# A fused attention and gated-MLP kernel: MLP groups reordered, their later steps emitted one to three groups behind, loads moved to a period's end, four result buffers for two

## Chip, cores and metric

One core of one Trainium2 chip. The metric is device microseconds of one execution of the whole kernel. Engines: PE (TensorE) multiplies, PEld loads its weights, DVE (VectorE), ACT (ScalarE) and POOL (GpSimd) do elementwise work, SP (SyncE) only issues DMAs. Each engine takes its instructions in the order in which they stand in its own queue, and waits on semaphores for those of other engines.

## What is computed

Block-causal attention over 8 batches and 8 heads (576 tokens, head size 64, blocks of 64 tokens), whose output is the input of a gated MLP with a spatial (token by token) product:

```python
scores = scale * np.matmul(q, k.transpose(0, 1, 3, 2))
scores = np.where(mask, scores, -1000000000.0)
attn = np.exp(scores - np.max(scores, axis=-1, keepdims=True))
attn = attn / (np.sum(attn, axis=-1, keepdims=True) + 1e-09)
x = np.matmul(attn, v)                       # then heads side by side: (batch, 576, 512)
h = np.maximum(x @ w_in, 0.0)                # w_in: 512 x 1024
u, v = (h[..., : d_ff // 2], h[..., d_ff // 2 :])
v_n = (v - mu) / np.sqrt(var + 1e-06)        # mean and variance over the 512 channels
v_s = np.einsum('ts,bsd->btd', w_spatial, v_n) + b_spatial[None, :, None]
out = (u * v_s) @ w_out                      # w_out: 512 x 512
```

## The kernel before

Attention is done in pairs of heads, four pairs to a batch, 32 in all. The first batch's four pairs run while the weights are prepared. From then on the program is a loop over the other 28 pairs, and one turn of it is called a **period** here: four periods to a batch, named first to fourth. In a period stand the scores of the pair (`scores_8` for the last 64 tokens, `scores_run` for the rest: matmul into PSUM, mask and maximum on DVE, L476, exponential on ACT, L483, scaling by the reciprocal sum on POOL, L497), the product with v of the pair before (`av_pair`, whose result is split into a rounded high part by ACT, L395, and a low part by DVE, L396), and the turning of this pair's probabilities: DVE transposes 32x32 blocks into `pb` (L556 to L565) and eight DMAs on SP regroup them into `ptt` (L574), for the next period's product.

Between these, PE works off a queue of **MLP groups** of the batch before (`moe`). A credit of `G_PAIR` per period says how many: one group after `scores_8`, the others behind `av_pair`, each followed by up to three steps of the turning. The operands are split into a high and a low fp32r part, and a product is made of three. A batch has 29 groups, each an accumulation in one of the two PSUM banks of `ps_m`:

- **v groups** (`mv`), 5: 128 tokens by 512 channels. ACT applies relu (L623), DVE makes mean and variance (L639, L640), ACT a logarithm and an exponential for the inverse root (L641, L642), DVE refines it (L643 to L655), ACT scales (L659) and casts the high part `vh` (L665), POOL makes the low part `vl` (L666). The fifth, the **tail group**, has the last 64 tokens, whose operand `xs` POOL copies together (`tail_evac`, L409), from both halves of all four pairs; its result is copied by ACT (L634), added by DVE (L635).
- **u groups** (`mu`), 8: two halves of the tokens (z) by four channel blocks; ACT applies relu into the tile `u` (L691).
- **spatial groups** (`ms`), 8: DVE multiplies the result by u (L716), ACT casts the high part `gh` (L717), POOL makes the low part `gl` (L718).
- **result groups** (`mo`), 8: ACT copies the result into a buffer `o` (L736), SP stores it.

With every group, all that follows its matmuls is written directly behind them. PE keeps the order written (every matmul is tied to the one before); on the other engines the framework's scheduler sets the order when the program is built, from its own estimates of when each instruction can run. The order of groups and the two loads of a later pair stand here:

```python
order = "vuvuvuvuvuuuu" if b else "v" * 5 + "u" * 8
groups = [(vs if w == "v" else us).pop(0) for w in order]
for z in range(2):
    groups += [(G_SP, lambda z=z, d=d: sp_group(z, d)) for d in range(ND)]
    groups += [(G_OUT, lambda z=z, e=e: out_group(z, e)) for e in range(NO)]
```

So the first period of a batch has the tail group first, then u and v groups by turns; the second the rest of v and u and one spatial group; the third three spatial groups of the first half, its four result groups, and one spatial group of the second half; the fourth the rest. The last batch's groups run alone at the end.

## Time and profile before

| | |
|---|---|
| runs (3) | 817.1, 817.97 (median), 818.67 us |
| profiled execution | 819.96 us, span 818.1 us |
| PE busy, matmuls | 718.9 us (88%) |
| DVE, ACT, POOL busy | 456.6, 383.7, 288.5 us |
| granted PE clock, mean | 0.954 |
| a batch's four periods | 99 us |
| regroup DMAs `ptt`, stores `outT`, loads of q and k, of v | 224, 64, 31, 32 |

How to read the lines below: in the list of waits, "PE mv L231 <- POOL xs L409: 24.4, 7, 4.0" says that PE stood idle 24.4 us, in 7 places, at most 4.0 us, before matmuls into `mv`, until POOL's instruction of line 409. In the timeline a row is start, duration, engine, line, operation, out<-in, form, count, and in brackets the idle time of its engine ahead of it and what ended that. Most matmuls are made by one helper, so their line is L231; the tile names tell them apart. Their durations overlap: starts, not durations, tell the rate.

### The profile page before, as it was taken

The page shows a single profiled execution, that of the slowest core. Times are in us where ns is not written, and L with a number is a line of the kernel's source. Part 1 is how long each engine was busy: PE and PEld are TensorE (multiplying, and loading weights), DVE is VectorE, ACT ScalarE, POOL GpSimd, SP SyncE. Part 2 cuts the span into 40 slices and gives each one's busy share as a digit, 9 for nine tenths or more (in the row PEclk, how much of TensorE's full clock was granted, in tenths as well). Part 3 has the DMA queues.
Part 4 walks back from the last instruction along what each step waited for, and adds up shares of the span by engine and source line. Part 5 has one row for each costly group of instructions (what it writes and reads, how often), then busy time and mean ns, then how long its engine had stood idle before and what let it go on. Part 6 is the DMA issues. An engine that isn't in the chain of part 4 may idle for free.

```text
span 818.1 us, 14375 instructions
## 1 busy us (share of the span) xinstructions
PE 718.9 (88%) x4864; PEld 609.0 (74%) x4864; DVE 456.6 (56%) x1739; ACT 383.7 (47%) x1088; POOL 288.5 (35%) x444
## 2 busy tenths in 40 slices
PE   8987898978989889888898798887987989879998
PEld 5545787767877678777787688776877868778897
DVE  7967763567525665356654555555654566535420
ACT  6776642446424564344543455343643447423532
POOL 5865543224313234232343313342142423323121
PEclk9999999989999999999999999999999999999999
DMA  5543564551446434463443534536346362353001
GB/s 201 170 143 102 156 172 114 148 136 51 124 112 165 118 83 120 112 166 87 114 118 100 157 81 128 141 79 160 92 97 157 97 165 70 81 126 93 18 8 51
DMA packets 53661, 94.42 MB, mean 115 GB/s; under 512 B 5970, under 2 KB 43346, under 8 KB 53588
## 3 DMA queue, kind: packets, MB, share of 16 engines
q1 hardware_dynamic: 53588, 93.52, 42.9%
q8 instruction: 38, 0.62, 0.3%
q14 instruction: 35, 0.29, 0.1%
HBM read 38.18 MB, written 9.44 MB: 58 GB/s over the span
## 4 chain that ended last, share of the span: by engine, by line
PE 36%; DVE 25%; ACT 11%; SPq 8%; DMA 8%; POOL 6%; issue 5%; DVEq 0%; POOLq 0%; ACTq 0%
PE mu L231 9%; SPq L574 8%; PE mv L231 8%; DVE pb L563 7%; ACT p L483 7%; DVE p L476 7%; PE ms L231 6%; DMA outT<-o 6%; PE s L231 5%; POOL p L497 5%; PE mo L231 4%; DVE sst L491 2%; DVE pb L556 2%; DVE x L396 2%; ACT vr L659 1%
## 5 line engine op out<-in xcount | busy, mean ns | idle before, releaser
L497 POOL TENSOR_SCALAR p<-p,sst 128x384 f32<-128x384 f32 (+4 forms) x252 | 137.0, 560 | 194.7 <-DVE sst L494 117.9
L483 ACT ACTIVATE p<-p,sst 128x384 f32<-128x384 f32 (+4 forms) x252 | 145.0, 577 | 53.6 <-DVE sst L476 52.4
L476 DVE CUSTOM_DVE_ANT_0 p<-s,mask 128x384 f32<-128x384 f32 (+4 forms) x252 | 114.3, 471 | 58.8 <-PE s L231 58.6
L231 PE MATMUL mu<-x,wi_hi 128*128 128x288 f32 x512 | 126.0, 328 | 17.2 <-ACT u L691 16.7
L231 PE MATMUL s<-raw 64*128 64x256 f32 (+4 forms) x640 | 126.5, 440 | 3.4 <-DVE nmax L291 1.8
L231 PEld LDWEIGHTS mu<-x,wi_hi 128*128 128x128 f32 x512 | 96.7, 215 | 21.2 <-ACT u L691 18.7
L716 DVE TENSOR_TENSOR u<-ms,u 128x288 f32<-128x288 f32 x64 | 28.0, 437 | 148.0 <-PE ms L231 148.0
L231 PEld LDWEIGHTS s<-raw 64*128 64x128 f32 (+1 forms) x640 | 73.2, 188 | 41.9 <-issue 19.8
L718 POOL TENSOR_TENSOR gl<-u,gh 128x288 fp32r<-128x288 f32 x64 | 51.4, 803 | 149.9 <-ACT gh L717 148.9
L563 DVE STREAM_TRANSPOSE pb<-p 128x384 f32<-128x384 f32 (+2 forms) x224 | 98.3, 455 | 8.7 <-POOL p L497 7.0
L231 PE MATMUL ms<-ws_hi,vh 128*128 128x288 f32 x256 | 83.8, 327 | 19.7 <-ACT o L736 19.7
L231 PE MATMUL mo<-gh,wo_hi 128*128 128x288 f32 x256 | 73.7, 308 | 23.0 <-DVE u L716 19.6
L231 PE MATMUL mv<-wi_hi,x 128*128 128x512 f32 x256 | 89.9, 414 | 3.4 <-ACT vr L623 3.3
L231 PE MATMUL av<-ptt,v 128*64 128x32 f32 (+4 forms) x1120 | 87.7, 306 | 2.8 <-DVE sst L476 2.7
L666 POOL TENSOR_TENSOR vl<-vr,vh 128x512 fp32r<-128x512 f32 x32 | 41.1, 1286 | 134.4 <-ACT vh L665 134.4
L231 PEld LDWEIGHTS av<-ptt,v 128*64 128x64 f32 x1120 | 75.6, 137 | 15.8 <-DVE sst L476 4.8
L736 ACT COPY o<-mo 128x288 f32<-128x288 f32 x64 | 25.4, 399 | 120.8 <-DMA outT<-o 64.9
L231 PE MATMUL ms<-ws_hi,vl 128*128 128x288 f32 x256 | 78.7, 308 | 0.0
L231 PE MATMUL ms<-ws_lo,vh 128*128 128x288 f32 x256 | 78.6, 307 | 0.0
L231 PE MATMUL mu<-x,wi_lo 128*128 128x288 f32 x256 | 77.9, 322 | 0.0
L717 ACT CAST gh<-u 128x288 fp32r<-128x288 f32 x64 | 27.6, 432 | 106.4 <-DVE u L716 106.4
L231 PE MATMUL mo<-gh,wo_lo 128*128 128x288 f32 x256 | 70.9, 297 | 0.0
(120 smaller groups left out, 1308.9 us busy)
## 6 DMA issues: line engine op xcount, KB each, us to landing
ptt<-pb SPq DMA_DIRECT2D x224, 200.0 KB, 4.1
raw<-qk SPq DMA_DIRECT2D x31, 608.0 KB, 4.0
v<-v SPq DMA_DIRECT2D x32, 320.0 KB, 3.0
outT<-o SPq DMA_DIRECT2D x64, 144.0 KB, 2.1
rwi<-w_in SPq DMA_DIRECT2D x8, 512.0 KB, 3.6
rwo<-w_out SPq DMA_DIRECT2D x4, 512.0 KB, 4.1
rws<-w_spT SPq DMA_DIRECT2D x4, 288.0 KB, 2.8
rwt<-w_spT SPq DMA_DIRECT2D x2, 144.0 KB, 4.2
```

The source lines that it names most:

```text
L231: ins = nc.tensor.matmul(out, lhsT, rhs, start=start, stop=stop).ins
L396: nc.vector.tensor_tensor(out=lo, in0=av, in1=hi.bitcast(F32), op=ALU.subtract)
L476: nc.vector.tensor_tensor_reduce(out=p[:, at:at + n], in0=ps, in1=mk, scale=-0.125, scalar=BIG if m == 0 else st[:, k:k + 1], op0=ALU.add, ...
L483: nc.scalar.activation(p, p, AF.Exp, bias=mx, scale=-1.0, accum_out=st[:, 10 + k:11 + k])
L497: nc.gpsimd.tensor_scalar(out=p, in0=p, scalar1=st[:, k:k + 1], scalar2=1.0, op0=ALU.mult, op1=ALU.mult)
L563: nc.vector.transpose(to(hd * XH + 32 * t, [[P, m], *dims] if m > 1 else dims), p[:, :m * P])
L574: nc.sync.dma_start(ptts[(b, pr)][:, a, xs], pb[32 * a:32 * a + 32, :, xs])
L666: nc.gpsimd.tensor_tensor(out=vl, in0=vr, in1=vh.bitcast(F32), op=ALU.subtract)
L716: nc.vector.tensor_tensor(out=uz, in0=ps[:, :HT], in1=uz, op=ALU.mult)
L717: nc.scalar.copy(gh[:, dc, :], uz)
L718: nc.gpsimd.tensor_tensor(out=gl[:, dc, :], in0=uz, in1=gh[:, dc, :].bitcast(F32), op=ALU.subtract)
L736: nc.scalar.copy(o, ps[:, :HT])
```

## The change

1. The v groups are made in the order 0, 1, tail, 2, 3 (before: tail, 0, 1, 2, 3). The last u group moves behind the four spatial groups of the first half.
2. Each group becomes a generator. When a group is issued, its matmuls and first step are emitted, and then every group still open advances by one step. So a v group's statistics, its root, and its scaling and casts are emitted one, two and three groups behind its relu; a spatial group's `gh` and `gl` one group behind its multiply, but for the fourth, which emits its cast at once and has its low part made by DVE.
3. A result group takes the last quarter of its inputs (k = 3) last, in all three products.
4. The loads of the next pair's v and of the second next pair's q and k stand at a period's end.
5. Four result buffers for two.

```diff
-    o_p = ctx.enter_context(tc.tile_pool(name="o_p", bufs=2))
+    o_p = ctx.enter_context(tc.tile_pool(name="o_p", bufs=4))
...
 # v_group
+            yield
             nc.vector.bn_stats(out=st[:m, 0:6], in_=vr[:m, :])
             nc.vector.bn_aggr(out=st[:m, 6:8], in_=st[:m, 0:6])
+            yield
             nc.scalar.activation(st[:m, 8:9], st[:m, 7:8], AF.Ln, bias=eps[:m, :])
...
+            yield
             nc.scalar.activation(
                 vr[:m, :], vr[:m, :], AF.Identity, bias=st[:m, 13:14], scale=st[:m, 12:13]
             )
...
 # u_group
             nc.scalar.activation(u_tile()[:, dc, zs], ps[:, :HT], AF.Relu)
+            yield
...
 # sp_group
             nc.vector.tensor_tensor(out=uz, in0=ps[:, :HT], in1=uz, op=ALU.mult)
+            if dc < ND - 1:
+                yield
             nc.scalar.copy(gh[:, dc, :], uz)
-            nc.gpsimd.tensor_tensor(
+            (nc.vector if dc == ND - 1 else nc.gpsimd).tensor_tensor(
                 out=gl[:, dc, :], in0=uz, in1=gh[:, dc, :].bitcast(F32), op=ALU.subtract
             )
+            if dc == ND - 1:
+                yield
...
 # out_group
-            for a, ws in ((gh, (wo_hi, wo_lo)), (gl, (wo_hi,))):
-                for k in range(ND):
-                    for w in ws:
+            for ks in (range(ND - 1), (ND - 1,)):
+                for a, w in ((gh, wo_hi), (gh, wo_lo), (gl, wo_hi)):
+                    for k in ks:
...
-        vs = [(G_V if c < FULL else G_VT, lambda c=c: v_group(c)) for c in (FULL, 0, 1, 2, 3)]
+        vs = [(G_V if c < FULL else G_VT, lambda c=c: v_group(c)) for c in (0, 1, FULL, 2, 3)]
...
-        for z in range(2):
-            groups += [(G_SP, lambda z=z, d=d: sp_group(z, d)) for d in range(ND)]
-            groups += [(G_OUT, lambda z=z, e=e: out_group(z, e)) for e in range(NO)]
+        groups = groups[:-1] + [(G_SP, lambda d=d: sp_group(0, d)) for d in range(ND)] + groups[-1:]
+        groups += [(G_OUT, lambda e=e: out_group(0, e)) for e in range(NO)]
+        groups += [(G_SP, lambda d=d: sp_group(1, d)) for d in range(ND)]
+        groups += [(G_OUT, lambda e=e: out_group(1, e)) for e in range(NO)]
...
+    def issue(f):
+        gen = f()
+        next(gen)
+        for e in list(behind):
+            if next(e, e) is e:
+                behind.remove(e)
+        behind.append(gen)
...
-            f()
+            issue(f)
...
-        if g + 1 < len(pairs):
-            load_v(*pairs[g + 1])
-        if g + 2 < len(pairs):
-            load_pair(*pairs[g + 2])
         n = max(n, g * NT)
         while group():
...
         for f in rest:
             f()
+        if g + 1 < len(pairs):
+            load_v(*pairs[g + 1])
+        if g + 2 < len(pairs):
+            load_pair(*pairs[g + 2])
```

How the change moves instructions shows in three places (names: tile, batch, number of the group; `x_4_3` is pair 3 of batch 4). First ACT in a batch's first period, from the split of the last pair's product on; before:

```order
L395 CAST x_4_3_4931<-av_4_3_0_4920 128x288
L395 CAST x_4_3_4931<-av_4_3_1_4934 128x288
L634 COPY vr_4_4_4953<-mv_4_4_4952 64x512
L691 ACTIVATE u_4_4998<-mu_4_0_0_4985 128x288
L641 ACTIVATE st_4_4_4954<-st_4_4_4954,eps_113 64x1
L642 ACTIVATE st_4_4_4954<-st_4_4_4954 64x1
L659 ACTIVATE vr_4_4_4953<-vr_4_4_4953,st_4_4_4954 64x512
L623 ACTIVATE vr_4_0_5008<-mv_4_0_5007 128x512
L672 CAST vs_a_123<-vr_4_4_4953 64x512
```

and now:

```order
L395 CAST x_4_3_4931<-av_4_3_0_4920 128x288
L395 CAST x_4_3_4931<-av_4_3_1_4934 128x288
L623 ACTIVATE vr_4_0_4949<-mv_4_0_4948 128x512
L643 ACTIVATE st_4_0_4950<-st_4_0_4950,eps_113 128x1
L694 ACTIVATE u_4_4984<-mu_4_0_0_4971 128x288
L644 ACTIVATE st_4_0_4950<-st_4_0_4950 128x1
L662 ACTIVATE vr_4_0_4949<-vr_4_0_4949,st_4_0_4950 128x512
L668 CAST vh_4_0_5036<-vr_4_0_4949 128x512
L623 ACTIVATE vr_4_1_4996<-mv_4_1_4995 128x512
```

The tail group's copy (L634) has left the place behind the split; v 0's relu stands there, u's relu now between the logarithm (L643) and the exponential (L644), and v 1's relu behind v 0's cast.

Next DVE in a third period, from the last row sums of the softmax on; before:

```order
L494 RECIPROCAL sst_4_2_4371<-sst_4_2_4371 128x4
L396 TENSOR_TENSOR x_4_1_4461<-av_4_1_0_4450,x_4_1_4461 128x288
L563 STREAM_TRANSPOSE pb_4_2_4500<-p1_4_2_0_4434 128x2x4x32
L396 TENSOR_TENSOR x_4_1_4461<-av_4_1_1_4464,x_4_1_4461 128x288
L563 STREAM_TRANSPOSE pb_4_2_4500<-p1_4_2_0_4434 128x4x32
L565 STREAM_TRANSPOSE pb_4_2_4500<-p3_4_2_1_4417 128x4x32
L563 STREAM_TRANSPOSE pb_4_2_4500<-p2_4_2_1_4427 128x3x4x32
L716 TENSOR_TENSOR u_3_4002<-ms_3_0_2_4482,u_3_4002 128x288
L563 STREAM_TRANSPOSE pb_4_2_4500<-p1_4_2_1_4439 128x2x4x32
L563 STREAM_TRANSPOSE pb_4_2_4500<-p1_4_2_1_4439 128x4x32
L716 TENSOR_TENSOR u_3_4002<-ms_3_0_3_4507,u_3_4002 128x288
```

and now:

```order
L494 RECIPROCAL sst_4_2_4373<-sst_4_2_4373 128x4
L565 STREAM_TRANSPOSE pb_4_2_4500<-p3_4_2_1_4419 128x4x32
L563 STREAM_TRANSPOSE pb_4_2_4500<-p2_4_2_1_4429 128x3x4x32
L563 STREAM_TRANSPOSE pb_4_2_4500<-p1_4_2_0_4436 128x2x4x32
L563 STREAM_TRANSPOSE pb_4_2_4500<-p1_4_2_0_4436 128x4x32
L563 STREAM_TRANSPOSE pb_4_2_4500<-p1_4_2_1_4441 128x2x4x32
L563 STREAM_TRANSPOSE pb_4_2_4500<-p1_4_2_1_4441 128x4x32
L720 TENSOR_TENSOR u_3_3988<-ms_3_0_3_4480,u_3_3988 128x288
L724 TENSOR_TENSOR gl_3_0_4334<-u_3_3988,gh_3_0_4333 128x288
L396 TENSOR_TENSOR x_4_1_4463<-av_4_1_0_4452,x_4_1_4463 128x288
L396 TENSOR_TENSOR x_4_1_4463<-av_4_1_1_4466,x_4_1_4463 128x288
```

The multiply of the fourth spatial group (L716, now L720) is behind the last transpose in both; the third's has gone ahead of them, and the two splits of x come behind the multiply and the new low part.

Last SP in a third period; before:

```order
L224 DMA raw_5_0_4480<-qk 128x1216
L248 DMA v_4_3_4478<-v 128x640
L574 DMA ptt_4_2_4527<-pb_4_2_4500 128x1x400 x8
L737 DMA outT<-o_3_0_0_4545 128x288
L737 DMA outT<-o_3_0_1_4565 128x288
L737 DMA outT<-o_3_0_2_4586 128x288
L737 DMA outT<-o_3_0_3_4602 128x288
```

and now:

```order
L574 DMA ptt_4_2_4523<-pb_4_2_4500 128x1x400 x7
L746 DMA outT<-o_3_0_0_4541 128x288
L574 DMA ptt_4_2_4523<-pb_4_2_4500 128x1x400
L746 DMA outT<-o_3_0_1_4561 128x288
L746 DMA outT<-o_3_0_2_4582 128x288
L746 DMA outT<-o_3_0_3_4598 128x288
L224 DMA raw_5_1_4857<-qk 128x1216
L248 DMA v_5_0_4855<-v 128x640
```

The loads have moved behind the stores; the first store stands ahead of the last regroup DMA.

## The prediction

> **What bounds the kernel now.** I read the page first, then TensorE's (PE's) waits, then the busy time by period, then the timeline around each wait.

> ```profile
> span 818.1 us, 14375 instructions
> PE 718.9 (88%) x4864; PEld 609.0 (74%) x4864; DVE 456.6 (56%) x1739; ACT 383.7 (47%) x1088; POOL 288.5 (35%) x444
> raw<-qk SPq DMA_DIRECT2D x31, 608.0 KB, 4.0
> ```
> ```profile
> PE mv L231 <- POOL xs L409: 24.4, 7, 4.0
> PE ms L231 <- ACT o L736: 19.7, 7, 3.3
> PE mo L231 <- DVE u L716: 19.6, 14, 2.4
> PE mu L231 <- ACT u L691: 16.7, 7, 2.7
> ```
> PE is the bound: no other engine passes 56%. What it loses stands in four waits, each once (the third twice) per batch: 80.4 us together. The next rows are one batch's four periods in PE's order: third, fourth, then first and second of the next batch (us of the period, then busy time of each engine, clock, DMA).

> ```profile
> 211.52:238.57 27.05, 22.70 (x167) 20.34 (x166) 11.87 (x47) 9.34 (x28) 8.31 (x14) 0.95 0.47 122
> 238.57:259.65 21.08, 19.53 (x151) 17.23 (x150) 11.97 (x47) 8.55 (x26) 8.32 (x14) 0.98 0.45 119
> 259.65:287.24 27.59, 23.48 (x142) 19.06 (x141) 17.36 (x65) 14.54 (x40) 6.42 (x11) 0.94 0.47 121
> 287.24:310.60 23.36, 20.95 (x148) 18.32 (x147) 14.26 (x55) 12.36 (x36) 8.96 (x13) 0.93 0.43 108
> ```
> A batch takes 99 us. The clock column is under 1 in all four, so I cut finer (PE busy, clock):

> ```profile
> 201.88:205.29 3.41, 1.01 (x8) 1.00 0.40 68
> 205.29:208.70 3.41, 3.41 (x17) 0.51 0.84 208
> 222.36:225.77 3.41, 2.10 (x16) 1.00 0.12 16
> 225.77:229.18 3.41, 3.19 (x23) 1.00 0.90 209
> 236.10:239.51 3.41, 3.41 (x14) 0.51 0.25 87
> 273.56:277.00 3.44, 3.44 (x13) 0.51 0.87 204
> ```
> A long wait costs twice: the 3.4 us behind it run at half clock, which loses about 1.6 us of matmuls. After a wait of 2.4 us (1.01 busy) it happens, after one of 1.3 us (2.10 busy) it doesn't. [...] The trace falls already after a window that was 30% busy. [...]

> **The change part by part.** A u group's 12 matmuls take 1.58 us and a v group's 2.77 (0.132 and 0.231 each); a spatial group's 14 are 1.85, the tail group's 8 are 1.85.

> ```profile
> 283.06 1.58 PE mu L231 x12
> 284.63 2.77 PE mv L231 x12
> ```

> *Four result buffers, reordered groups: the third period.*

> ```profile
> 224.06 6.80 SPq L574 DMA_DIRECT2D ptt<-pb  x8
> 224.61 0.42 DVE L716 TENSOR_TENSOR u<-ms,u 128x288 f32<-128x288 f32 x1
> 225.18 0.37 PE L231 MATMUL mo<-gh,wo_hi 128*128 128x288 f32 x1 [1.31 <-DVE u L716]
> 225.50 0.42 DVE L716 TENSOR_TENSOR u<-ms,u 128x288 f32<-128x288 f32 x1
> 227.56 0.29 PE L231 MATMUL mo<-gh,wo_hi 128*128 128x288 f32 x1
> 230.97 5.19 SPq L737 DMA_DIRECT2D outT<-o  x4
> 234.92 0.79 ACT L736 COPY o<-mo 128x288 f32<-128x288 f32 x2 [5.19 <-DMA outT<-o]
> 235.37 0.40 PE L231 MATMUL ms<-ws_hi,vh 128*128 128x288 f32 x1 [2.83 <-ACT o L736]
> ```
> The third result's copy waits for a buffer, the buffer for its store, the store for eight regroup DMAs ahead of it on SP. With four buffers no copy waits inside a batch half, and the next half comes a period later: the 2.83 us go, and the half clock at 236.10. The 1.31 us wait is another: the first result group needs a PSUM bank, and the multiply that frees it stands behind the block transposes on DVE. The change puts a u group (1.58) where a spatial group (1.85) was, but the bank is now that of the fourth spatial group, whose multiply (225.50) is last of all; only what is taken from ahead of it, a multiply and x's subtraction (0.3 to 0.8), brings it forward, less where DVE waits for POOL. I take the start as it was, 225.2 (bounds 224.9 and 225.6), so this wait stays. Then the group runs through in 1.58 instead of 227.56 - 225.18 = 2.38, since its last quarter comes last and DVE makes the low half. Four result groups and one spatial: 225.2 + 6.32 + 1.85 = 233.4, against 238.57: 5.2 us, and 0.45 more for the half clock that reached past 238.57. **Third period: -5.65** (bounds -3.5, if the half clock stays behind the wait that is left, and -7.1 if that wait is gone too).

> *Fourth period*: the same order around the products, so its wait stays; the first result group gains from its last quarter, 0.5 (0 to 0.8). **-0.5.**

> *Tail group third: the first period.*

> ```profile
> 262.46 0.78 ACT L736 COPY o<-mo 128x288 f32<-128x288 f32 x2 [5.33 <-DMA outT<-o]
> 263.14 0.78 ACT L483 ACTIVATE p<-p,sst 128x576 f32<-128x576 f32 x1
> 268.98 0.67 ACT L395 CAST x<-av 128x288 fp32r<-128x288 f32 x2
> 271.43 0.86 DVE L563 STREAM_TRANSPOSE pb<-p 128x384 f32<-128x384 f32 x2
> 272.07 0.51 PE L231 MATMUL mv<-wi_hi,xs 128*128 128x512 f32 x1 [3.75 <-POOL xs L409]
> 272.84 0.58 ACT L634 COPY vr<-mv 64x512 f32<-64x512 f32 x1 [3.20 <-PE mv L231]
> 273.46 0.69 DVE L635 TENSOR_TENSOR vr<-mv,vr 64x512 f32<-64x512 f32 x1 [1.18 <-ACT vr L634]
> ```
> The first v group now needs of the last pair only the first cast at 268.98, at its seventh matmul. That cast comes earlier too: ACT's copies no longer wait 5.33 us for a store, which let the period's first exponential start only at 263.14. How much earlier lies between 0 and 5.33; the nearest row is DVE's own work ahead of the cast, which stays, so I take 0.8. The cast's first half (0.34) is then done at 268.5, and the seventh matmul starts there, not at 272.07: the six ahead of it ended at 272.07 - 3.75 = 268.3, or a little sooner, so the wait is half a microsecond and brings no half clock. Six matmuls of 0.231 later, at 269.9, v ends. What is late next is ACT, which takes its rows in order: relu, logarithm, u's relu, the square root's exponential, scale, cast, and only then the next v's relu. The last batch, where nothing else runs, shows this loop:

> ```profile
> 770.73 0.59 ACT L623 ACTIVATE vr<-mv 128x512 f32<-128x512 f32 x1
> 771.30 0.41 ACT L691 ACTIVATE u<-mu 128x288 f32<-128x288 f32 x1
> 772.30 0.29 ACT L641 ACTIVATE st<-st,eps 128x1 f32<-128x1 f32 x1 [0.58 <-DVE st L640]
> 775.05 0.59 ACT L623 ACTIVATE vr<-mv 128x512 f32<-128x512 f32 x1
> ```
> Relu to logarithm 1.57, logarithm to next relu 2.75; u's relu is hidden behind the statistics there and now stands inside: +0.41. The first v's statistics follow the block transposes (end 272.5), logarithm at 273.5, next relu at 276.65, done 277.25; PE is ready for the tail group, which needs that bank, at 269.9 + 1.58 + 2.77 + 1.58 = 275.8: a new wait of 1.45. Next, v 2 needs the tail group's bank: ACT's copy at 276.65 + 1.57 + 0.41 + 2.1 = 280.75 (the cast, 0.6, is behind it), copy and DVE's add end at 282.05; PE is ready at 277.25 + 1.85 + 1.58 = 280.7: a new wait of 1.35. v 2 ends at 284.8, where it ended at 287.24. **First period: -2.4** (bounds -5.4 without the two waits, and +0.8 if both pass 1.9 us and bring a half clock).

> *Second period.*

> ```profile
> 204.19 0.29 ACT L641 ACTIVATE st<-st,eps 128x1 f32<-128x1 f32 x1 [3.95 <-DVE st L640]
> 204.84 0.40 PE L231 MATMUL mu<-x,wi_hi 128*128 128x288 f32 x1 [2.40 <-ACT u L691]
> ```
> PE waits for u's relu, which stands on ACT behind the logarithm, which waits for statistics that DVE makes after the transposes. The rows stand so after the change too, so this wait and its half clock stay. DVE gets the tail's two splits (about 1.1) at the period's start, and ACT's scale and cast of v 2 leave the exponentials (1.4): **+0.2** (-3.9, wait and half clock gone, to +0.8).

> *The rest.* Loads at the period's end: the same 63 loads, each with a whole period (over 20 us) before its use, against 4.0 us to land; SP's stores and regroup DMAs no longer stand behind them. Nothing, unless a load comes a period late (below). Each half's last low part on DVE: 16 subtractions of about 0.44 in place of POOL's; behind them wait the splits of x, not due for a period. Nothing.

> Sum per batch: -5.65 - 0.5 - 2.4 + 0.2 = -8.35. Batches 1 to 6 run so, beside the attention of the next: -50. Batch 0, among the weights' preparation, has the same waits at other sizes: half of that, -4 (0 to -8.4). Batch 7, alone, has none of the four waits now, and its ACT loop grows from 775.05 - 770.73 = 4.32 to 4.73 against PE's 4.35 for a v and a u group: 0 (-1 to +2). Together -54. The profiled execution took 819.96, 1.9 over its span of 818.1; the median of the runs is 817.97, and 817.97 - 54 = **764 us**.

> **Rivals.** [...] (2) ACT's line is shorter than I make it and the first period's two waits vanish, 6 x 2.8: 747; with the second period's wait gone too, 724. For it: later steps are emitted one to three groups behind; against: the order on ACT, where they stand in the same row. (3) The first period's waits grow past 1.9 us and bring half clocks, 6 x 3.2 = 19: 783. (4) The stores stay the gate: the copies wait again a half later. Then the third period keeps 5.2 of its 5.65: 795. Against: the store issued at 230.97 had landed at 234.92, and its buffer is needed a period, over 20 us, later. (5) **Slower**: a load at the period's end comes late, and every period's first scores wait for it. There are 27 periods; the gain is gone when each waits 2.0 us, that is, when a load lands 22 us after the end of the period before its own; at 3 us each it would be 845. Against: 4.0 us to land.

> **Chances.** My sum 0.55, (1) 0.08, (2) 0.15, (3) 0.12, (4) 0.05, (5) 0.05. A difference under 0.2% (1.6 us) is no change by what such a measurement can tell. Faster 0.94, same 0.01, slower 0.05. The range, 740 to 788, takes in (1), (3) and the nearer half of (2).

> **What would show it.** Right: ACT's results wait for no store; PE's spatial groups for no copy; PE's v groups not for the tail split; half clock once per batch, in the second period; new waits of PE's v groups on ACT's relu and on DVE's add, over 1 us each; the wait on DVE's multiply still there, twice per batch. Wrong: half-clock stretches as many as before, or none; waits on loads; a second period that shortens.

## The result, and the profile after

The changed kernel takes 748.1 us (median of 4, 746.6 to 749.89) against 817.54 before (4 runs): ratio 0.9153, interval 0.9124 to 0.9183, so 8.5% faster. The profiled execution took 749.12 us. The page's first lines after, the head of PE's list of waits, and the four periods of the same batch in the same order as before (third, fourth, then first and second):

```profile
span 747.3 us, 14409 instructions
PE 691.7 (93%) x4864; PEld 583.6 (78%) x4864; DVE 464.9 (62%) x1755; ACT 383.8 (51%) x1088; POOL 276.4 (37%) x428
```
```profile
PE mo L231 <- DVE u L720: 19.9, 14, 2.4
PE mv L231 <- DVE vr L635: 9.9, 8, 3.9
PE mu L231 <- ACT u L694: 8.9, 7, 1.3
PE ms L231 <- ACT u L694: 3.5, 8, 1.5
```
```profile
205.05:226.78 21.73, 20.36 (x164) 18.66 (x163) 12.14 (x47) 9.25 (x28) 6.87 (x13) 1.00 0.49 127
226.78:247.25 20.47, 19.06 (x153) 17.16 (x152) 12.30 (x48) 9.06 (x27) 7.53 (x13) 1.00 0.53 140
247.25:270.34 23.09, 21.99 (x142) 17.46 (x141) 16.44 (x60) 13.21 (x37) 7.70 (x12) 1.00 0.56 149
270.34:292.35 22.01, 20.37 (x149) 17.60 (x148) 15.16 (x61) 13.38 (x38) 8.36 (x13) 1.00 0.45 119
```

A batch takes 87.3 us where it took 99. Two of the four waits are gone from the list (POOL's `xs`, ACT's copy of a result), the wait on u's relu is 1.3 us at most where it was 2.7, the wait on DVE's multiply is as it was. The clock column is 1.00 in all four periods: in each of them a wait of 0.9 to 1.4 us is left, and none brings a half clock. By period, from the start of the first score matmul to the next one's, mean of six batches (the fourth: of five), before to after:

| | predicted | measured |
|---|---|---|
| third period | -5.65 | -5.6 |
| fourth period | -0.5 | -0.5 |
| first period | -2.4 | -4.6 |
| second period | +0.2 | -1.3 |
| all up to the end of batch 0's groups | -4 | +0.7 |
| batch 7 with the last fourth period | -0.5 | -0.1 |

In the row of batch 0, the time up to the third pair's scores is 1.2 us longer (26.56 us for 25.34). That stretch takes 25.0 to 26.7 us in the twelve profiled executions, and differs by 1.1 between the kernel before and the same kernel with four buffers. The rest of the row is 0.5 us shorter.

### The profile page after: what moved, and what is told of

Same layout as the page of the kernel before. It is cut to its first block, busy times and chain, and to the rows that moved or that the text cites. A ratio compares the mean times of both kernels' runs of the same rounds, so it can differ in the third digit from the quotient of the medians.

```text
span 747.3 us, 14409 instructions
## 1 busy us (share of the span) xinstructions
PE 691.7 (93%) x4864; PEld 583.6 (78%) x4864; DVE 464.9 (62%) x1755; ACT 383.8 (51%) x1088; POOL 276.4 (37%) x428
## 4 chain that ended last, share of the span: by engine, by line
DVE 39%; PE 25%; ACT 16%; POOL 8%; issue 6%; DMA 3%; SPq 3%; POOLq 0%; DVEq 0%; ACTq 0%
PE mo L231 12%; DVE pb L563 9%; DVE p L476 8%; ACT p L483 7%; PE ms L231 6%; POOL p L497 4%; DVE st L640 3%; PE s L231 3%; ACT vr L662 3%; SPq L574 2%; DVE pb L556 2%; POOL vl L669 2%; PE mv L231 2%; DVE sst L491 1%; DVE vr L636 1%
## 5 line engine op out<-in xcount | busy, mean ns | idle before, releaser
L497 POOL TENSOR_SCALAR p<-p,sst 128x384 f32<-128x384 f32 (+4 forms) x252 | 136.2, 557 | 203.3 <-DVE sst L494 101.5
L483 ACT ACTIVATE p<-p,sst 128x384 f32<-128x384 f32 (+4 forms) x252 | 145.0, 577 | 47.6 <-DVE sst L476 44.6
L231 PE MATMUL s<-raw 64*128 64x256 f32 (+4 forms) x640 | 127.6, 446 | 2.3 <-DVE nmax L291 1.8
L231 PE MATMUL mu<-x,wi_hi 128*128 128x288 f32 x512 | 113.2, 300 | 8.9 <-ACT u L694 8.9
L231 PEld LDWEIGHTS s<-raw 64*128 64x128 f32 (+1 forms) x640 | 73.6, 191 | 41.0 <-issue 23.3
L231 PE MATMUL mv<-wi_hi,x 128*128 128x512 f32 x256 | 90.2, 414 | 12.5 <-DVE vr L635 9.9
L563 DVE STREAM_TRANSPOSE pb<-p 128x384 f32<-128x384 f32 (+2 forms) x224 | 96.2, 452 | 5.6 <-POOL p L497 4.4
L231 PEld LDWEIGHTS mu<-x,wi_hi 128*128 128x128 f32 x512 | 85.4, 188 | 12.6 <-ACT u L694 10.5
L720 DVE TENSOR_TENSOR u<-ms,u 128x288 f32<-128x288 f32 x64 | 28.2, 441 | 100.3 <-PE ms L231 100.2
L231 PE MATMUL av<-ptt,v 128*64 128x32 f32 (+4 forms) x1120 | 86.8, 306 | 2.3 <-DVE sst L476 2.1
L231 PEld LDWEIGHTS av<-ptt,v 128*64 128x64 f32 x1120 | 77.0, 137 | 13.5 <-DVE sst L476 4.6
L231 PE MATMUL ms<-ws_hi,vh 128*128 128x288 f32 x256 | 80.8, 316 | 3.6 <-ACT u L694 3.5
L231 PE MATMUL ms<-ws_hi,vl 128*128 128x288 f32 x256 | 76.2, 298 | 1.0 <-POOL vl L669 0.3
L724 POOL TENSOR_TENSOR gl<-u,gh 128x288 fp32r<-128x288 f32 x48 | 38.4, 801 | 100.5 <-ACT gh L723 100.5
L231 PE MATMUL mo<-gh,wo_hi 128*128 128x288 f32 x256 | 56.9, 303 | 19.9 <-DVE u L720 19.9
L231 PE MATMUL ms<-ws_lo,vh 128*128 128x288 f32 x256 | 75.3, 294 | 0.0
L231 PEld LDWEIGHTS mv<-wi_hi,x 128*128 128x128 f32 x256 | 49.2, 192 | 28.6 <-DVE vr L635 11.9
L231 PE MATMUL mu<-x,wi_lo 128*128 128x288 f32 x256 | 69.8, 295 | 0.0
## 6 DMA issues: line engine op xcount, KB each, us to landing
raw<-qk SPq DMA_DIRECT2D x31, 608.0 KB, 3.8
```

The lines of the kernel that those rows point to most:

```text
L231: ins = nc.tensor.matmul(out, lhsT, rhs, start=start, stop=stop).ins
L483: nc.scalar.activation(p, p, AF.Exp, bias=mx, scale=-1.0, accum_out=st[:, 10 + k:11 + k])
L497: nc.gpsimd.tensor_scalar(out=p, in0=p, scalar1=st[:, k:k + 1], scalar2=1.0, op0=ALU.mult, op1=ALU.mult)
L563: nc.vector.transpose(to(hd * XH + 32 * t, [[P, m], *dims] if m > 1 else dims), p[:, :m * P])
L720: nc.vector.tensor_tensor(out=uz, in0=ps[:, :HT], in1=uz, op=ALU.mult)
L724: (nc.vector if dc == ND - 1 else nc.gpsimd).tensor_tensor(out=gl[:, dc, :], in0=uz, in1=gh[:, dc, :].bitcast(F32), op=ALU.subtract)
```

## The experiments

Each was timed beside the kernel before on the same chip, and ratios are against that. Between chips the kernel before moved by 0.4%, so small differences are read from the periods, not from medians taken on different chips.

**Two result buffers again.**

```diff
-    o_p = ctx.enter_context(tc.tile_pool(name="o_p", bufs=4))
+    o_p = ctx.enter_context(tc.tile_pool(name="o_p", bufs=2))
```

> The changed kernel with two result buffers again (everything else as changed). Theory A (the stores gate the result copies whenever there are two buffers): the third copy of each half waits again for the first store, which stands behind seven or eight regroup DMAs on SP; PE then waits for that copy in the third period (1.5 to 3 us) and ACT's first exponential comes late at the start of the first period; 2 to 4 us a batch, six batches: 760 to 772 us, take 765, and a wait of PE's spatial group on ACT's copy is back in the list. Theory B (the loads' move and the store ahead of the last regroup DMA have freed the stores, buffers don't matter): 748 us, no such wait.

782.18 us, ratio 0.9564 (0.9512 to 0.9616): 34 us of the gain are gone, and the wait on the copy is back. From PE's list of waits:

```profile
PE ms L231 <- ACT o L745: 16.1, 7, 3.1
PE av L231 <- DVE sst L476: 7.3, 9, 1.2
PE mv L231 <- ACT x L395: 6.7, 6, 1.3
```

Theory A, larger than expected. By the waits, one late store delays three things: the third period's spatial group (2 to 3 us), and at the start of the next first period, through ACT's late exponentials, the product with v (1 us) and the first v group (1.1 us). The third period is 2.3 to 5.0 us longer, the first 1.6 to 2.4.

**Four buffers alone**, in the kernel before.

```diff
-    o_p = ctx.enter_context(tc.tile_pool(name="o_p", bufs=2))
+    o_p = ctx.enter_context(tc.tile_pool(name="o_p", bufs=4))
```

> The kernel before with four result buffers and nothing else changed. Theory A (the buffers alone take the store out of the copies' way, and with it the delay of the exponentials at the start of the first period): the 2.83 us wait of the third period goes with its half clock (4.4 us a batch), and the first period's last cast comes 1.6 us earlier, so its wait for xs falls from 3.75 to about 2.2 us: 6 us a batch, 782 us, no wait on the copy of a result in the list. Theory B (the loads ahead of the stores on SP hold the stores up too, so that four buffers alone do little): 800 us or more, the wait still there. If the first period keeps its 3.75 us: 791 us.

782.27 us, ratio 0.9525 (0.9496 to 0.9553), as theory A had it. No wait on a copy is left. The wait on `xs` is 2.9 us at most where it was 4.0:

```profile
PE mv L231 <- POOL xs L409: 18.6, 7, 2.9
PE mu L231 <- ACT u L691: 17.5, 11, 2.7
```

So one number in one line brings about half of the gain, with everything else as before. That the time met the forecast is partly luck. The wait on `xs` fell to 2.9 us and not to 2.2. And the wait of the second period stayed (2.4 us, 2.7 in one batch), yet its half clock went in four batches of six, while three fourth periods got one behind the 1.33 us wait that brought none before: a matter of where a wait falls (last section).

**The tail group first again.**

```diff
-        vs = [... for c in (0, 1, FULL, 2, 3)]
+        vs = [... for c in (FULL, 0, 1, 2, 3)]
```

> The changed kernel with the v groups in the order tail, 0, 1, 2, 3 again. Theory A (the tail group first costs its wait for POOL's copy of xs): the wait is back, shorter than the 3.75 us of before by the 1.6 us that the last split now comes earlier, so about 2.2 us, with a half clock behind it (1.6 us), less the 0.93 us wait that the third place costs: +2.9 us in each of six batches, -3 us in batch 0 whose 3.9 us wait on the tail's result goes: 762 us. Theory B (the lag alone gave the gain in the first period, the place of the tail group nothing): 745 to 750 us. If the wait comes out under 1.9 us and brings no half clock: 750 us.

761.34 us, ratio 0.9311 (0.9269 to 0.9353). Theory A: first periods longer by 2.7 to 4.0 us, second ones shorter by 0.5 to 0.6, and the wait back, at 2.8 to 3.1 us where I expected 2.2.

```profile
PE mv L231 <- POOL xs L409: 19.0, 7, 3.1
```

**No lag in the v groups** (the spatial groups keep theirs; taking that away alone was not tried).

```diff
# v_group
-            yield
             nc.vector.bn_stats(out=st[:m, 0:6], in_=vr[:m, :])
...
-            yield
             nc.scalar.activation(st[:m, 8:9], st[:m, 7:8], AF.Ln, bias=eps[:m, :])
...
-            yield
             nc.scalar.activation(
                 vr[:m, :], vr[:m, :], AF.Identity, ...
...
+            yield          # at the very end of the group
```

> The changed kernel with the v groups' statistics, root, scale and casts emitted directly behind their relu again (spatial groups keep their lag). Theory A (in the second period the third v group's scale and cast stand among the exponentials again, POOL then makes its low part while DVE adds the softmax's epsilon, and that instruction of DVE takes 1.1 us instead of 0.2): PE's wait for u's relu in the second period goes from 1.31 to about 2.3 us and brings back its half clock: 2.6 us in each of six batches, 763 us, clock 0.975. Theory B (the second period's wait got shorter for another reason, such as the loads' move or the u group moved out of it): 746 to 750 us, wait 1.3 us, no half clock.

760.87 us, ratio 0.9313 (0.9273 to 0.9354): 13 us, which the second periods account for (1.7 to 3.2 us each). The wait and its half clock are back, but not for the reason that I gave. In the timeline of a second period POOL makes the low part `vl` ahead of two scalings, and DVE's transposes wait for these; its row L491 takes under 0.2 us there (the longest of the run, 0.66, is in batch 0):

```profile
281.98 1.31 POOL L666 TENSOR_TENSOR vl<-vr,vh 128x512 fp32r<-128x512 f32 x1
283.25 1.16 POOL L497 TENSOR_SCALAR p<-p,sst 128x384 f32<-128x384 f32 x2
283.89 1.04 DVE L563 STREAM_TRANSPOSE pb<-p 128x384 f32<-128x384 f32 x2 [1.03 <-POOL p L497]
289.40 0.41 PE L231 MATMUL mu<-x,wi_hi 128*128 128x288 f32 x1 [2.72 <-ACT u L692]
```

**The same, with only POOL's low part late** (edit against the run without the lag). The low part is emitted three groups later, and that of v 2 stands behind the scalings; the tail group's last copies move one group with it. This parts POOL's share from ACT's, whose scale and cast stand among the exponentials in both. The helper `after` adds an order between two instructions of one engine and no semaphore; `scaled` lists the scalings of L497.

```diff
                 nc.scalar.copy(vh, vr)
-                nc.gpsimd.tensor_tensor(out=vl, ...)
                 vn[c] = (vh, vl)
+                for _ in range(3):
+                    yield
+                low = nc.gpsimd.tensor_tensor(out=vl, ...).ins
+                if c == 2 and b > 0:
+                    after(low, scaled[-1])     # order only: behind the last scaling (L497)
```

> As the run without the lag of the v groups (their statistics, root, scale and cast directly behind the relu), but the low part of v 2 stands on POOL behind the scaling of the probabilities of the second period. ACT keeps the scale and the cast among the exponentials. Theory A (POOL's low part, 1.3 us, ahead of the scaling is what makes the block transposes and so the statistics late): the 2.72 us wait of the second period falls to 1.3 to 1.6 us and its half clock goes: 746 to 750 us. Theory B (ACT's 1.4 us of scale and cast among the exponentials do it): the wait stays at 2.7 us with its half clock, 761 us.

751.0 us, ratio 0.9182 (0.9154 to 0.9211). The scalings now run ahead of `vl`, and PE waits 1.76 us:

```profile
276.15 2.49 POOL L505 TENSOR_SCALAR p<-p,sst 128x512 f32<-128x512 f32 x4 [0.99 <-DVE sst L502]
281.96 1.26 POOL L677 TENSOR_TENSOR vl<-vr,vh 128x512 fp32r<-128x512 f32 x1
283.92 0.40 PE L231 MATMUL mu<-x,wi_hi 128*128 128x288 f32 x1 [1.76 <-ACT u L704]
```

Nearer to theory A, though wait and time lie just outside its ranges (1.3 to 1.6 us, 746 to 750), and a half clock still follows the same wait in two batches of six. Of the 1.4 us between 2.72 and the changed kernel's 1.31, about 1.0 goes with POOL's low part. I put the 0.45 that is left down to ACT's two steps; no run shows that alone.

**Loads where they were.**

```diff
+        if g + 1 < len(pairs):
+            load_v(*pairs[g + 1])
+        if g + 2 < len(pairs):
+            load_pair(*pairs[g + 2])
         n = max(n, g * NT)
         while group():
...
-        if g + 1 < len(pairs):
-            load_v(*pairs[g + 1])
-        if g + 2 < len(pairs):
-            load_pair(*pairs[g + 2])
     while queue:
```

> The changed kernel with the loads of q, k and v where they stood before the change (ahead of the MLP groups of a period). Theory A (the loads' place is worth nothing, each has a period to spare): 748 us, within 2. Theory B (the loads hold up the regroup DMAs and stores behind them on SP): 752 to 765 us, with waits of PE's product on regroup DMAs or of result copies on stores.

746.86 us, ratio 0.9145 (0.91 to 0.9189); no period of batches 1 to 6 differs by more than 0.06 us from the changed kernel's. Theory A: this part is worth nothing.

**The u group not moved.**

```diff
-        groups = groups[:-1] + [(G_SP, lambda d=d: sp_group(0, d)) for d in range(ND)] + groups[-1:]
+        groups += [(G_SP, lambda d=d: sp_group(0, d)) for d in range(ND)]
```

> The changed kernel with the last u group back in its place ahead of the spatial groups. Theory A (the u group covers the time in which DVE gets to the fourth spatial group's multiply): the third period's first result group then comes 1.58 us earlier and has to wait about as much longer for its last quarter, 1.2 us after its nine first matmuls are taken off; with the half clock 2.9: 755 to 766 us, take 758, longer waits on DVE's multiply or low part in the third period. Theory B (the multiply is not what the group waits for, or comes earlier with the group ahead of it gone): 748 us.

745.43 us, ratio 0.9078 (0.9053 to 0.9103). A third and a second period of this run:

```profile
288.43:310.72 22.29, 20.96 (x166) 19.04 (x165) 12.34 (x48) 9.36 (x28) 7.55 (x13) 1.00 0.50 132
267.10:288.43 21.33, 19.85 (x148) 17.32 (x146) 14.71 (x60) 13.33 (x38) 7.73 (x12) 1.00 0.45 115
```

The third is 0.55 longer, the second 0.65 shorter: 0.1 us a batch in favour of not moving it. Theory A is wrong. The first result group does not come earlier without the u group: the credit hands out as many groups per period, a spatial group moves into the free place, and the wait on the multiply stays (1.30 us). That the whole comes out 0.8% below the changed kernel by ratio is not explained by the periods of batches 1 to 6. Most of it lies at the program's start: from the first score matmul to the third pair's the profiled execution took 21.3 us against 22.7, and the stretch that holds batch 0's v groups 35.5 against 37.0. In the other runs that share these stretches the first took 21.1 to 22.8, the second 34.7 to 38.0, so a cause in the edit is not shown.

**The result groups' old order of products, low part on POOL.**

```diff
-            for ks in (range(ND - 1), (ND - 1,)):
-                for a, w in ((gh, wo_hi), (gh, wo_lo), (gl, wo_hi)):
-                    for k in ks:
+            for a, ws in ((gh, (wo_hi, wo_lo)), (gl, (wo_hi,))):
+                for k in range(ND):
+                    for w in ws:
...
-            (nc.vector if dc == ND - 1 else nc.gpsimd).tensor_tensor(
+            nc.gpsimd.tensor_tensor(
```

> The changed kernel with the result groups' products in the old order (the last quarter not last) and the last low part on POOL again. Theory A (the prediction's 0.5 us in the fourth period and 0.8 in the third come from this): 0.5 to 0.8 us in two periods of each batch, 752 to 757 us, the first result group of a half takes longer than 1.6 us. Theory B (the first result group starts so late that all its inputs are there): 748 us.

752.0 us, ratio 0.915 (0.9123 to 0.9177): not told apart from the changed kernel by time. By periods, the third is the same within 0.06 us in five batches of six (0.24 shorter in the sixth). The fourth is 0.2 to 0.5 longer, and 1.7 in one batch, where a half clock follows (20.74 against 20.36 in another, by the windows of this run and of the changed kernel):

```profile
311.93:332.67 20.74, 19.20 (x152) 17.12 (x151) 11.94 (x47) 8.96 (x27) 8.35 (x14) 1.00 0.53 141
```
```profile
314.07:334.43 20.36, 19.04 (x153) 17.16 (x152) 12.33 (x48) 8.96 (x27) 7.52 (x13) 1.00 0.50 138
```

Both theories in part: A in the fourth period, where PE now also waits 0.2 us for ACT's `gh`, B in the third. The order of products and the low part on DVE were undone together, so their shares are not known.

**The waits that are left, taken away by order alone.** In each period the transposes of the last four blocks stand behind the first short DVE step that PE waits for.

```diff
+    def mark(ins):
+        if armed[0]:               # set at the start of each period's groups
+            hold[0], armed[0] = ins, False
...
+        if t < 2 and hold[0] is not None:
+            after(ins, hold[0])    # transposes of blocks 1 and 0, in turn_blocks
...
-            nc.vector.bn_aggr(out=st[:m, 6:8], in_=st[:m, 0:6])
+            mark(nc.vector.bn_aggr(out=st[:m, 6:8], in_=st[:m, 0:6]).ins)
...
-            nc.vector.tensor_tensor(out=uz, in0=ps[:, :HT], in1=uz, op=ALU.mult)
+            mark(nc.vector.tensor_tensor(out=uz, in0=ps[:, :HT], in1=uz, op=ALU.mult).ins)
...
+            if c == 1:
+                after(scaled, copied[-1])   # ACT: scale of v 1 behind the copy of the tail's result
```

> The changed kernel with an order forced on DVE and ACT: in each period the last four block transposes (of two or one blocks of 128) stand behind the first statistics or multiply that follows the product with v, and on ACT the scaling of v 1 stands behind the copy of the tail group's result. Theory A (the waits of PE that are left, 0.93, 1.31 + 0.17, 1.37 and 1.32 us per batch, are waits for DVE's transposes ahead of short steps, and for ACT's scaling ahead of a copy): nearly all 5.1 us go, 30 us in six batches and some in batch 0: 716 us, and the regroup DMAs, started up to 1 us later, still land a period ahead of their use. Theory B (the wait only moves: to the root's chain on ACT, to the low part of the last quarter, or to the regroup DMAs): 735 us or more.

724.2 us, ratio 0.8824 (0.8779 to 0.8868). The second and third periods lose 1.5 us each, the fourth 0.1 to 0.5; the first changes by +0.4 to -1.2, since the wait on the cast, 0.3 us at most in the changed kernel, has grown there. The head of PE's list (the longest waits of the first, third and fourth line are batch 0's):

```profile
PE ms L231 <- ACT u L717: 4.1, 8, 1.5
PE mv L231 <- ACT x L395: 4.1, 6, 1.3
PE mv L231 <- DVE vr L656: 3.9, 1, 3.9
PE mo L231 <- DVE u L743: 3.5, 8, 0.9
```

The time lies between the two forecasts. Theory A for most of it, B in the first period: the cast of the last pair's split stands on ACT behind the exponentials.

**One step further.**

```diff
# x_evac, last pair of a batch
+        if pr == NPAIR - 1 and b < B - 1 and exps:
+            for e in exps[-2:]:
+                after(e, cast)     # the last two exponentials behind the cast
...
-        vs = [... for c in (0, 1, FULL, 2, 3)]
+        vs = [... for c in ((0, 1, FULL, 2, 3) if b else (0, 1, 2, 3, FULL))]
...
-            if c == 1:
+            if c == 1 and b:
```

> The version with the forced order on DVE and ACT (724 us), with two more steps: in the first period the last two exponentials stand behind the casts of the product's result on ACT, and in batch 0 the tail group is the last of the v groups. Theory A (the 0.83 us wait of the first period on that cast goes, and in batch 0 the 3.9 us wait with its half clock): 6 x 0.8 + 3.9 + 1.6 = 10 us, 714 us. Theory B (the waits move to the first statistics and to ACT's relus): 720 to 726 us.

716.9 us, ratio 0.8761 (0.8734 to 0.8788), the fastest version here. PE is busy 96% of the span (691 of 719 us), and the largest waits in its list stand once, in batch 0; what is left on DVE's multiply are eight waits, under 0.5 us each outside batch 0:

```profile
PE 690.9 (96%) x4864; PEld 580.9 (81%) x4864; DVE 454.1 (63%) x1755; ACT 384.6 (53%) x1088; POOL 276.8 (38%) x428
PE mv L231 <- ACT vr L648: 3.9, 5, 3.2
PE mo L231 <- DVE u L747: 3.9, 8, 1.2
PE ms L231 <- DVE u L747: 2.8, 1, 2.8
```

The first period's wait on the cast is gone; in batch 0 the wait only moved, from the tail's result (3.9 us) to ACT's relu (3.2) and a multiply (2.8). So theory A holds in the first period and B in batch 0. The profiled executions of the two versions, 721.1 and 719.1 us long, differ by less than their medians, which come from two chips.

## Why the prediction came out as it did

The time lay in the range, and the main mechanism held: PE's waits on stores and on the tail's split went, and the half clocks behind them. But the gain was 70 us where the sum said 54. Two periods came out as forecast, one term was too small, and two had the wrong sign. Two of the prediction's own signs of being wrong came: no half clock is left in batches 1 to 7, where it kept one in each second period, and the second period shortened. Of the two new waits that it forecast, on ACT's relu and on DVE's add, only the second came, at 0.93 us.

- *Third and fourth period: right.* Stores no longer hold copies (64.9 us of ACT's waits before, none after), the half clock at the end of the third is gone, the wait on DVE's multiply stays, and the fourth period's 0.5 comes with the order of products and the low part on DVE (0.2 to 0.5 by their experiment, without the batch with the half clock). In the third period the number was right with one reason wrong: I put 0.8 us down to these two, but with both undone the period is as long. There PE waits for the fourth multiply, and by then its other inputs are there. The multiply, 12.9 us into the period, still stands behind the last transpose:

```profile
217.94 0.42 DVE L720 TENSOR_TENSOR u<-ms,u 128x288 f32<-128x288 f32 x1
218.51 0.63 PE L231 MATMUL mo<-gh,wo_hi 128*128 128x288 f32 x3 [1.37 <-DVE u L720]
```

- *First period: the term was mis-sized, -2.4 for -4.6.* The step that failed is "the first v's statistics follow the block transposes (end 272.5)". I let the cast come 0.8 us earlier, of bounds 0 and 5.33, and left the transposes where they were, though both follow from the same exponentials. The cast came 1.56 us earlier in its period (268.98 - 259.65 = 9.33; 255.02 - 247.25 = 7.77) and the transposes' end 1.45 (from 12.64 to 11.19 or so, at 258.44). So all of ACT's line that I counted from 272.5 was earlier: v 1's relu, which I had 17.0 us into the period, started at 15.0 (0.4 of it because the line itself was shorter than I made it). It was done just as PE came, and the tail group's 1.45 us wait never arose. The wait of v 2 did, 0.93 for 1.35. The earlier cast comes with the buffers: with two of them again the first period is 1.6 to 2.4 us longer.

```profile
255.02 0.67 ACT L395 CAST x<-av 128x288 fp32r<-128x288 f32 x2
258.44 0.64 DVE L640 BATCH_NORM_STATS2 st<-vr 128x6 f32<-128x512 f32 x1
262.23 0.59 ACT L623 ACTIVATE vr<-mv 128x512 f32<-128x512 f32 x1
267.51 0.50 PE L231 MATMUL mv<-wi_hi,x 128*128 128x512 f32 x1 [0.93 <-DVE vr L635]
```

- *Second period: the term was wrong, +0.2 for -1.3.* "The rows stand so after the change too" holds for ACT and DVE. POOL's order there was not in my argument. Before, in the timeline of a second period, and after:

```profile
296.20 1.30 POOL L666 TENSOR_TENSOR vl<-vr,vh 128x512 fp32r<-128x512 f32 x1
296.43 1.10 DVE L491 TENSOR_SCALAR sst<-sst 128x2 f32<-128x2 f32 x1
300.38 1.62 POOL L497 TENSOR_SCALAR p<-p,sst 128x256 f32<-128x256 f32 x4 [1.27 <-DVE sst L494]
302.27 0.65 DVE L639 BATCH_NORM_STATS2 st<-vr 128x6 f32<-128x512 f32 x1
```
```profile
281.46 1.62 POOL L497 TENSOR_SCALAR p<-p,sst 128x256 f32<-128x256 f32 x4 [0.72 <-DVE sst L494]
283.05 1.30 POOL L669 TENSOR_TENSOR vl<-vr,vh 128x512 fp32r<-128x512 f32 x1
284.53 0.65 DVE L640 BATCH_NORM_STATS2 st<-vr 128x6 f32<-128x512 f32 x1
286.07 0.40 PE L231 MATMUL mu<-x,wi_hi 128*128 128x288 f32 x1 [1.31 <-ACT u L694]
```

  The lag puts `vl` behind the scalings on POOL. The statistics come 0.8 us earlier in the period (284.53 - 270.34 = 14.2; 302.27 - 287.24 = 15.0), and PE comes to the wait 0.2 later. So the wait fell from 2.40 to 1.31 us, which no longer brings a half clock. A spatial group in place of a u group (0.27 us) and two new waits, 0.17 and 0.15 us by the profile but 0.8 us together by the starts of the matmuls around them, give part of it back.
- *Batch 0: +0.7 for -4, outside its bounds; -0.5 without the program's start.* The tail group as third of five v groups in a row made PE wait 3.9 us for DVE's add of its result (until 83.72), with half clock from 82.13 to 88.96. With the tail first that stretch was 2.8 us shorter.
- *The rest: right.* Loads are worth nothing, batch 7 with the period ahead of it changed by 0.1.

Of the rivals, (2) came nearest: the tail's wait went, as it says, and 747 was its number, but the wait of v 2 stayed, the second period gave 1.5 us a batch more than the sum said, and batch 0 gave less; that the total came to 747 is luck. (1) in the chances and the range, a half clock made by something else than PE's waits, is shown by no run: none is left in batches 1 to 7 of the changed kernel, where the waits of PE are gone or 1.4 us at most. (3) and (4) did not come; with two buffers a good part of (4) comes, 2.3 to 5.0 us in each third period. (5) is refuted by the loads' own experiment.

Taken one at a time, undoing the buffers costs 34 us, the tail's place 13, the v groups' lag 13, the loads, the u group and the order of products nothing that the times can tell. The lag of the spatial groups was not tried alone and stays open.

## What to carry to other kernels

When one step is moved earlier, move everything in the sum that hangs on the same source, and read the queue of every engine on the way to the wait: about 1.0 us on POOL (2.72 to 1.76 us of waiting when only the low part moved) decided a wait that the profile books to ACT. Where a wait ends at a short step standing behind long ones on its engine, an order between those two alone can take it away: that brought another 24 us on top of the change, and 31 with the second step, with no work removed. A buffer count is the cheapest thing to try alone, and here it was half of the gain.

## What the hardware showed

```profile
228.95:232.36 3.41, 2.32 (x18) 1.00 0.93 239
232.36:235.78 3.42, 2.30 (x16) 1.00 0.48 139
413.26:416.68 3.42, 1.75 (x14) 1.00 0.92 231
416.68:420.09 3.41, 3.00 (x19) 1.00 0.36 118
505.43:508.84 3.41, 1.36 (x11) 1.00 0.84 212
508.84:512.25 3.41, 2.32 (x9) 0.50 0.37 130
601.00:604.41 3.41, 0.81 (x7) 1.00 0.86 209
604.41:607.82 3.41, 3.41 (x14) 0.50 0.32 110
```

The first wait (2.21 us) is split between two windows and brings no half clock; the second (2.08) leaves its window 51% busy; the third and fourth leave 40% and 24%, and the clock falls. No run shows a limit of 1.9 us per wait, which lies between the 1.3 and 2.4 us of the prediction's windows; a share of a window fits the counts better. By the step of the grid a wait of 1.5 us leaves 56% of its window busy if the rest of it is (an estimate, 1.91 of 3.41 us), and behind no window over 55% did the clock fall. Two short waits did it together: with four buffers alone, a fourth period's wait of 1.33 us and the one of 0.22 behind it lay within one window in three batches, which left it 55% busy (1.86 us), and the clock fell in these three; in the other three the second reached past the window's end, and it didn't. In the same run the second period's 2.43 us wait was split between two windows in three batches, with no half clock behind.

A small DVE instruction was long beside one of POOL: in the kernel before, L491, 0.16 us as a median, took 1.08 to 1.11 in each of the six second periods (1.10 at 296.43) and ended within 0.03 us of POOL's `vl` (297.50 there). Whether POOL's instruction held it is not shown by a run that changes only that, and whether it delayed the old second period stays open too, since the run without the lag shows the same wait without the stretch.
